# Softmax sums with their 1e-9 beside them, the gate as a second factor, u w by a product with ones, and new places for all steps

## The chip, the core and the metric

One Trainium2 chip, one of its cores: TensorE (PE, with its weight loads shown as PEld), VectorE (DVE), ScalarE (ACT), GpSimd (POOL) and SyncE (SP, which issues every DMA of this kernel). The metric is the device time of one execution in microseconds (us). Before the change three timed runs gave 396.64, 402.85 and 397.48 us; the median is 397.48 us.

## The reference

Two layers. The first is a linear attention with decay, for B=4, H=8, S=768, D=48:

```python
cur = np.einsum('bhd,bhe->bhde', u[None] * kt, vt)
y[:, :, t] = np.einsum('bhd,bhde->bhe', rt, state + cur)
state = w[None, :, :, None] * state + np.einsum('bhd,bhe->bhde', kt, vt)
```

The second takes y as x (4 x 768 x 384) and runs 4 expert attentions with heads of 64, of which each token uses the best two by a gate:

```python
a = np.exp(scores)
a /= a.sum(-1, keepdims=True) + 1e-09
ye = a @ v @ wo[e]
...
w = np.exp(sel)
w /= w.sum(-1, keepdims=True) + 1e-09
```

The scores are causal, and the wq and wk of the test are large, so products of q and k are made of two parts (hi and lo) each.

## The kernel before

The sequence of each of the 4 batches is cut into 6 chunks of 128 tokens: chunk n runs from 0 to 23, and n % 6 = 5 is the last of a batch. Three chunks make a group G (0 to 7), two groups make a batch; g = G % 2 is 0 for a batch's first half and 1 for its second, whose attention also reads the keys of the first.

Work on a chunk (names begin with a_): `load_chunk` fetches k and r into kdbuf (4 buffers) and rdbuf (3), `load_vh` and `load_zv` fetch v in two layouts. `a_decay` (L230) multiplies k and r by the decay tables tab_k and tab_r, on DVE for the first 3 chunks and on GpSimd for the others. `a_own` forms the u-term: two products on GpSimd into ku (L238, L239), a sum on DVE (L241), and two halves of ownv (L244, one on DVE and one on GpSimd). `a_transpose` (L253, L256, L257), `a_scores` (L265, L267), `a_out` (L277, L279) and `a_state` (L288, then zs on DVE at L294 and zvbuf on GpSimd at L296, twice, for the two 64-token halves) make the chunk's output and carry the state. `a_xt` (L307 to L310) turns the output round and splits it.

Work on a group (names begin with m_): `m_proj` (L337, xq at L341 to L345, then SP copies into tk at L355 and tq at L351), `m_values` (L366), `m_gate`, and for each of 4 experts and 3 query chunks `m_scores` (L412, L413): DVE takes minima over the masked scores (L418), ACT the exponential and its row sum (L419). After the third query chunk the factor f is made on DVE (L423 adds 1e-9, L424 inverts, L425 multiplies by the gate) and GpSimd scales the three tiles pr by it (L429). `m_turn` (L437, L439) transposes them, `m_av` (L453) multiplies by the values, `m_out` (L469 to L473) by wo.

Order: the table ORDER gives every step a place in units of one group; the steps are issued in order of these places (`at`), `needs` only asserts that what a step reads was issued before, and the tile framework's scheduler puts each engine's instructions in line from there. At run time each engine works strictly through its own line, and SP issues its DMAs in line too, so a transfer whose buffer is not free holds back all transfers behind it. PSUM has four banks named ps, taken in turn by every step that uses one (a_state's and m_av's among them), and two pairs named psb for the scores.

Before the first chunk, powers of w are built on DVE (L156 to L160), copied into two tiles (DVE L169, ACT L170), transposed by PE (L173) and copied into tab_k and tab_r by ACT (L174). `load_uw` spreads w and u over all 128 partitions by two DMAs of 192 KB and multiplies them on DVE (L184).

Of the kernel before, what the change touches and what calls it, by code (L numbers as in the profile page):

```python
# [7 lines left out]
F32 = mybir.dt.float32  # L8
F32R = mybir.dt.float32r
BF16 = mybir.dt.bfloat16  # L10
AF = mybir.ActivationFunctionType
OP = mybir.AluOpType
AX = mybir.AxisListType
PSUM = bass.MemoryType.PSUM

ORDER = {
    "load": -0.6596, "decay": -0.4545, "late": 0.0159, "early": 0.2138, "early_project": -0.0623, "copy_zv":
    -0.2698, "load_uw": -1.0607, "load_vh": -0.5828, "load_zv": -0.7408, "transpose": -0.2149, "own": -0.1496,
    "burst": -0.0903, "xt": 0.3275, "project": 0.0765, "project_step": 0.0977, "attend": [-0.0676, -0.1006],
    "av": [0.2761, 0.2103], "mix": [0.3321, 0.4911], "mix_step": 0.1117, "load_qk": -0.2109, "load_v":  # L20
    -0.6283, "load_o": 0.3769, "attend_step": 0.0365, "values": 0.2328, "tail": -0.0092, "tail_step": 0.9545,
}
# [12 lines left out]
def decay_attention_then_mixture_of_attention(  # L35
# [27 lines left out]
    GC = 3  # L63
# [3 lines left out]
    scale = 0.125  # L67
# [70 lines left out]
    for i, rows in enumerate((lo, hi)):  # L138
# [27 lines left out]
    tab_k = const.tile([P, H, 64], F32, name="tab_k")  # L166
    for nat, half in ((tab_k, up[:, :, 63::-1]), (tab_r, down[:, :, 64:0:-1])):
        col = work.tile([P, S], F32, name="pr", bufs=BUFS["pr"])[:, :NP * C].rearrange("d (p c) -> d p c", p=NP)
        nc.vector.tensor_copy(col[:, :, :64], half)  # L169
        nc.scalar.activation(col[:, :, 64:], half, AF.Copy)  # L170
        pst = ps1.tile([P, NP, P], F32, name="ps")
        for p in range(NP):
            nc.tensor.transpose(pst[:, p, :], col[:, p, :], ident)  # L173
        nc.scalar.activation(nat.rearrange("s h d -> s (h d)"), pst.rearrange("s p d -> s (p d)"), AF.Copy)  # L174
    w64 = const.tile([P, NP, 1], F32, name="w64")
    nc.vector.tensor_copy(w64, up[:, :, 64:65])

    uw = const.tile([P, H, D], F32, name="uw")

    def load_uw():  # L180
        wb = work.tile([P, H, D], F32, name="ku", bufs=BUFS["ku"])
        nc.sync.dma_start(wb, bass.AP(tensor=w.tensor, offset=w.offset, ap=[[0, P], [1, H * D]]))
        nc.sync.dma_start(uw, bass.AP(tensor=u.tensor, offset=u.offset, ap=[[0, P], [1, H * D]]))
        tc.keep_in_program_order(nc.vector.tensor_tensor(uw, uw, wb, op=OP.mult))  # L184


    wqk_hi = const.tile([P, KT, 2 * NV], F32R, name="wqk_hi")
# [36 lines left out]
    xt = {}  # L224
# [85 lines left out]
        nc.vector.tensor_tensor(lo[:, :, cols], ps, hi[:, :, cols].bitcast(F32), op=OP.subtract)  # L310


    keys = {}
    mg = {}

    def m_start(G):
        b, g = divmod(G, NG)
        keys[b, g] = dict(
            tk=work.tile([P, E, GT], F32R, name="tk", bufs=3),
            vv=work.tile([P, GC, E, HD], F32, name="vv", bufs=3),  # L320
        )
        mg[G] = dict(
            tq=[work.tile([P, 2, GT], F32R, name="tq", bufs=BUFS["tq"]) for _ in range(E)],
            sums=tiny.tile([P, E, GC], F32, name="sums"),
        )

    def m_proj(G, kind, pr):
# [74 lines left out]
    def m_scores(G, e, j):  # L402
        b, g = divmod(G, NG)
        tq, sums = mg[G]["tq"], mg[G]["sums"]
        N = (g * GC + j + 1) * C
        psb = ps2.tile([P, 1024], F32, name="psb")
        q = slice(j * C, (j + 1) * C)
        for h in range(g + 1):
            tk = keys[b, h]["tk"]
            n = GT if h < g else (j + 1) * C  # L410
            o = psb[:, 128 + h * GT:128 + h * GT + n]
            nc.tensor.matmul(o, tq[e][:, 0, q], tk[:, e, :n], start=True, stop=False)  # L412
            nc.tensor.matmul(o, tq[e][:, 1, q], tk[:, e, :n], start=False, stop=True)  # L413
        ps = psb[:, 128:128 + N]

        nm = tiny.tile([P, 1], F32, name="nm", bufs=6)
        pr = work.tile([P, S], F32, name="pr", bufs=BUFS["pr"])
        nc.vector.tensor_tensor_reduce(pr[:, :N], ps, after[:, S - N:], 1.0, 3e38, op0=OP.add, op1=OP.min, accum_out=nm)  # L418
        nc.scalar.activation(pr[:, :N], pr[:, :N], AF.Exp, bias=nm, scale=-1.0, accum_out=sums[:, e, j:j + 1])  # L419
        mg[G]["p", e, j] = pr  # L420
        if j == GC - 1:
            f = tiny.tile([P, GC], F32, name="f", bufs=4)
            nc.vector.tensor_scalar(f, sums[:, e, :], 1e-9, None, op0=OP.add)  # L423
            nc.vector.reciprocal(f, f)  # L424
            nc.vector.tensor_tensor(f, f, mg[G]["gate"][:, :, e], op=OP.mult)  # L425
# [170 lines left out]
```

## Time and profile before

| what | value |
|---|---|
| median of 3 runs | 397.48 us (396.64 to 402.85) |
| the profiled execution's own time | 399.55 us |
| its span, first to last instruction | 397.8 us |
| PE busy | 352.7 us (89%) |
| DVE, ACT, POOL busy | 260.5, 239.6, 228.1 us |
| mean granted TensorE clock | 0.961 of full speed |

Busy times overlap, and a busy PE is not PE at its peak: its matmuls are pipelined and their records overlap. The granted clock is 1.0 (2.4 GHz) or 0.5 (1.2 GHz) in each stretch. The view of waits names, for an engine and line, what ended its idle time; such idle time costs something only where the engine, or one that waits for it, sets the pace. The profiled execution lies 2.07 us above the median.

### The profile page before, as it was taken

What the parts mean: (1) busy time and instruction counts of PE and PEld (TensorE: products, weight loads), DVE (VectorE), ACT (ScalarE), POOL (GpSimd) and SP (SyncE); (2) the same over time, 40 slices, a digit from 0 to 9 for tenths busy, and PEclk for the clock granted to TensorE, in tenths of its full rate; (3) what the DMA queues carried; (4) which work ended last, traced back from release to release, by engine and by line L of the source; (5) the groups of instructions that cost most, each with busy time, mean ns of one, the idle gap of its engine ahead of it and who ended that gap; (6) DMA issues with size and microseconds to landing.
All of it is one profiled execution on the core that took longest, in us unless ns stands there. A gap on an engine that the chain in (4) does not pass through costs nothing.

```text
span 397.8 us, 10483 instructions
## 1 busy us (share of the span) xinstructions
PE 352.7 (89%) x3762; PEld 303.1 (76%) x3762; DVE 260.5 (65%) x728; ACT 239.6 (60%) x597; POOL 228.1 (57%) x322
## 2 busy tenths in 40 slices
PE   4566798779987999899889999999789999999995
PEld 1465687669866997599768997699668998798863
DVE  7598689567687766676677757675577655447510
ACT  0868637253764675656557485657468485557961
POOL 5389997867389628674497826773465503213420
PEclk9669999689999999999989999999989999999999
DMA  8995376917943774536844582536811550074011
GB/s 122 179 178 97 71 164 147 143 33 162 175 83 70 172 174 75 103 81 138 173 97 95 134 207 63 98 82 140 180 51 31 133 130 22 7 172 123 20 41 59
DMA packets 114772, 43.95 MB, mean 110 GB/s; under 512 B 102945, under 2 KB 110625, under 8 KB 114721
## 3 DMA queue, kind: packets, MB, share of 16 engines
q1 hardware_dynamic: 114720, 43.28, 52.9%
q8 instruction: 30, 0.49, 0.5%
q14 instruction: 22, 0.17, 0.1%
HBM read 19.67 MB, written 4.72 MB: 61 GB/s over the span
## 4 chain that ended last, share of the span: by engine, by line
PE 53%; DMA 7%; DVE 6%; ACT 4%; POOL 3%; issue 3%; SPq 3%; ACTq 0%; DVEq 0%; POOLq 0%
PE ps L337 10%; PE ps L453 9%; PE ps L437 8%; PE psb L412 4%; PE ps L277 4%; PE psb L413 3%; PE ps L366 3%; DMA kdbuf<-in_k_dram 3%; PE ps L265 3%; PE ps L288 2%; PE ps L253 2%; SPq L351 2%; PE ps L469 2%; PE ps L470 2%; PE ps L471 2%
## 5 line engine op out<-in xcount | busy, mean ns | idle before, releaser
L429 POOL TENSOR_SCALAR pr<-pr,f 128x128 f32<-128x128 f32 (+5 forms) x96 | 60.9, 652 | 68.7 <-DVE f L425 22.6
L419 ACT ACTIVATE pr<-pr,nm 128x128 f32<-128x128 f32 (+5 forms) x96 | 64.3, 671 | 32.9 <-DVE nm L418 31.3
L418 DVE CUSTOM_DVE_ANT_0 pr<-psb,after 128x128 f32<-128x128 f32 (+5 forms) x96 | 58.9, 619 | 33.2 <-PE ps L437 27.2
L439 ACT ACTIVATE pt<-ps 128x384 f32<-128x384 f32 x144 | 56.4, 421 | 31.1 <-PE ps L437 29.1
L437 PE MATMUL ps<-ident,pr 128*128 128x128 f32 x336 | 59.9, 282 | 8.2 <-POOL pr L429 3.3
L296 POOL TENSOR_TENSOR zvbuf<-zs,w 64x192 f32<-64x192 f32 x88 | 47.1, 535 | 13.6 <-DVE zs L294 9.4
L437 PEld LDWEIGHTS ps<-ident,pr 128*128 128x128 f32 x336 | 40.0, 141 | 16.2 <-POOL pr L429 5.0
L412 PE MATMUL psb<-tk,tq 128*128 128x128 f32 (+2 forms) x144 | 50.0, 351 | 2.1 <-DVE nm L418 1.1
L453 PE MATMUL ps<-pt,vv 128*64 128x384 f32 (+2 forms) x288 | 42.8, 436 | 6.1 <-DVE zs L294 6.1
L294 DVE TENSOR_TENSOR zs<-ps,zvbuf 64x192 f32<-64x192 f32 x88 | 31.0, 353 | 21.3 <-POOL zvbuf L296 16.0
L413 PE MATMUL psb<-tk,tq 128*128 128x128 f32 (+2 forms) x144 | 43.1, 316 | 0.0
L230 POOL TENSOR_TENSOR kdbuf<-kdbuf,tab_k 128x384 f32<-128x384 f32 x21 | 21.7, 1034 | 35.0 <-DMA kdbuf<-in_k_dram 32.1
L453 PEld LDWEIGHTS ps<-pt,vv 128*64 128x64 f32 x288 | 20.2, 141 | 26.8 <-issue 16.7
L267 DVE TENSOR_TENSOR rabuf<-ps,before 64x512 f32<-64x512 f32 x48 | 33.0, 688 | 4.1 <-PE ps L265 3.2
L337 PE MATMUL ps<-xt_hi,wqk_hi 128*128 128x384 f32 x96 | 35.0, 364 | 0.8 <-ACT xt_hi L309 0.7
L337 PE MATMUL ps<-xt_lo,wqk_hi 128*128 128x384 f32 x96 | 33.3, 347 | 1.1 <-DVE xt_lo L310 1.1
L238 POOL TENSOR_TENSOR ku<-kdbuf,uw 128x384 f32<-128x384 f32 x24 | 25.7, 1072 | 14.7 <-DVE kdbuf L230 9.1
L341 ACT ACTIVATE xq<-ps 128x384 fp32r<-128x384 f32 x32 | 15.6, 488 | 30.2 <-PE ps L337 24.4
L277 PE MATMUL ps<-zvbuf,rabuf 128*64 128x48 f32 x768 | 29.3, 227 | 4.6 <-POOL ku L239 3.2
L337 PE MATMUL ps<-xt_hi,wqk_lo 128*128 128x384 f32 x96 | 32.8, 342 | 0.0
L277 PEld LDWEIGHTS ps<-zvbuf,rabuf 128*64 128x64 f32 x768 | 26.4, 141 | 8.0 <-POOL ku L239 3.8
L412 PEld LDWEIGHTS psb<-tk,tq 128*128 128x128 f32 x144 | 27.8, 193 | 5.3 <-DVE nm L418 3.1
(109 smaller groups left out, 817.4 us busy)
## 6 DMA issues: line engine op xcount, KB each, us to landing
tq<-xq SPq DMA_DIRECT2D x64, 192.0 KB, 3.4
tk<-xq SPq DMA_DIRECT2D x64, 96.0 KB, 2.2
kdbuf<-in_k_dram SPq DMA_DIRECT2D x24, 192.0 KB, 4.0
rdbuf<-in_r_dram SPq DMA_DIRECT2D x24, 192.0 KB, 3.9
vhbuf<-in_v_dram SPq DMA_DIRECT2D x48, 96.0 KB, 3.1
out_dram<-o SPq DMA_DIRECT2D x23, 192.0 KB, 2.3
zvbuf<-in_v_dram SPq DMA_DIRECT2D x72, 48.0 KB, 2.5
pr<-in_moe_wv_dram SPq DMA_DIRECT2D x3, 128.0 KB, 3.6
```

Source lines behind the costliest of these rows:

```text
L267: nc.vector.tensor_tensor(ra[rows, par].rearrange("s i p t -> s (i p) t"), ps[rows].rearrange("s i p t -> s (i p) t"), before[rows, None, ...
L277: nc.tensor.matmul(ps[half, 2 * p + par, :], ra[:, par, i, p, :], zv[:, par, i, p, :], start=True, stop=True)
L296: nc.gpsimd.tensor_tensor(zvbuf[(n + i) % NZ][rows, par, 1 - i], zs[rows], w64[rows].to_broadcast([64, NP, D]), op=OP.mult)
L337: nc.tensor.matmul(ps, a[:, t, m0:m0 + P], x[:, t, :], start=i == 0, stop=i == n - 1)
L412: nc.tensor.matmul(o, tq[e][:, 0, q], tk[:, e, :n], start=True, stop=False)
L413: nc.tensor.matmul(o, tq[e][:, 1, q], tk[:, e, :n], start=False, stop=True)
L418: nc.vector.tensor_tensor_reduce(pr[:, :N], ps, after[:, S - N:], 1.0, 3e38, op0=OP.add, op1=OP.min, accum_out=nm)
L419: nc.scalar.activation(pr[:, :N], pr[:, :N], AF.Exp, bias=nm, scale=-1.0, accum_out=sums[:, e, j:j + 1])
L429: nc.gpsimd.tensor_scalar(p[:, :N], p[:, :N], f[:, i:i + 1], 1.0, op0=OP.mult, op1=OP.mult)
L437: nc.tensor.transpose(pst[:, j, :], mg[G]["p", e, j][:, i * C:(i + 1) * C], ident)
L439: nc.scalar.activation(pt[:, j0:], pst[:, j0:], AF.Copy)
L453: nc.tensor.matmul(psy[par * HD:par * HD + HD, j0 * C:], vv[:, i % GC, e, :], mg[G]["t", e, i][:, j0:].rearrange("s j t -> s (j t)"), star ...
```

## The change

Line numbers of the changed kernel differ: L429 becomes L444, L230 becomes L240, L238 and L239 become L248 and L249, L244 becomes L254, L296 becomes L306, L170 is gone, L174 becomes L177, L118 becomes L119. The 1e-9 stands in a second column beside each softmax sum, so one sum over two columns replaces the addition of a constant; the gate is no longer multiplied into f but handed to GpSimd as the second factor of the scaling. Both columns of the decay tables are copied by DVE. A copy of a small tile (lower) is put first on ACT. u w is formed in one partition and spread by a matmul with ones. Every number of the table ORDER changes; two of its lines are shown, with the numbers that place the u-term (own), the output and state (burst, with a_out a third of a group behind it) and the turned output (xt).

```diff
 ORDER = {
...
-    -0.2698, "load_uw": -1.0607, "load_vh": -0.5828, "load_zv": -0.7408, "transpose": -0.2149, "own": -0.1496,
-    "burst": -0.0903, "xt": 0.3275, "project": 0.0765, "project_step": 0.0977, "attend": [-0.0676, -0.1006],
...
+    -0.3428, "load_uw": -0.9439, "load_vh": -0.5687, "load_zv": -0.6948, "transpose": -0.2504, "own": 0.1079,
+    "burst": -0.0679, "xt": 0.4025, "project": 0.1361, "project_step": 0.0927, "attend": [-0.0751, -0.2394],
...
+    nc.scalar.activation(lower.rearrange("p a b -> p (a b)"), lower.rearrange("p a b -> p (a b)"), AF.Copy)
...
-        nc.vector.tensor_copy(col[:, :, :64], half)
-        nc.scalar.activation(col[:, :, 64:], half, AF.Copy)
+        for i in range(2):
+            nc.vector.tensor_copy(col[:, :, i * 64:i * 64 + 64], half)
...
-        nc.scalar.activation(nat.rearrange("s h d -> s (h d)"), pst.rearrange("s p d -> s (p d)"), AF.Copy)
+        behind(nc.scalar.activation(nat.rearrange("s h d -> s (h d)"), pst.rearrange("s p d -> s (p d)"), AF.Copy))
...
+    ones = const.tile([1, P], F32, name="ones")
+    nc.gpsimd.memset(ones, 1.0)
     def load_uw():
-        wb = work.tile([P, H, D], F32, name="ku", bufs=BUFS["ku"])
-        nc.sync.dma_start(wb, bass.AP(tensor=w.tensor, offset=w.offset, ap=[[0, P], [1, H * D]]))
-        nc.sync.dma_start(uw, bass.AP(tensor=u.tensor, offset=u.offset, ap=[[0, P], [1, H * D]]))
-        tc.keep_in_program_order(nc.vector.tensor_tensor(uw, uw, wb, op=OP.mult))
+        row = tiny.tile([1, 2, H * D], F32, name="row", bufs=1)
+        nc.sync.dma_start(row[:, 0], w.rearrange("h d -> (h d)")[None, :])
+        nc.sync.dma_start(row[:, 1], u.rearrange("h d -> (h d)")[None, :])
+        tc.keep_in_program_order(nc.vector.tensor_tensor(row[:, 0], row[:, 0], row[:, 1], op=OP.mult))
+        ps = ps1.tile([P, H * D], F32, name="ps")
+        nc.tensor.matmul(ps, ones, row[:, 0], start=True, stop=True)
+        nc.scalar.activation(uw.rearrange("p h d -> p (h d)"), ps, AF.Copy)
...
+    sumsbuf = [const.tile([P, E, GC, 2], F32, name=f"sums{i}") for i in range(2)]
+    for t in sumsbuf:
+        nc.gpsimd.memset(t[:, :, :, 1:], 1e-9)
...
-        nc.scalar.activation(pr[:, :N], pr[:, :N], AF.Exp, bias=nm, scale=-1.0, accum_out=sums[:, e, j:j + 1])
+        nc.scalar.activation(pr[:, :N], pr[:, :N], AF.Exp, bias=nm, scale=-1.0, accum_out=sums[:, e, j, 0:1])
...
-            f = tiny.tile([P, GC], F32, name="f", bufs=4)
-            nc.vector.tensor_scalar(f, sums[:, e, :], 1e-9, None, op0=OP.add)
+            f = tiny.tile([P, GC, 1], F32, name="f", bufs=4)
+            nc.vector.tensor_reduce(f, sums[:, e], axis=AX.X, op=OP.add)
             nc.vector.reciprocal(f, f)
-            nc.vector.tensor_tensor(f, f, mg[G]["gate"][:, :, e], op=OP.mult)
+            gate = mg[G]["gate"]
...
-                nc.gpsimd.tensor_scalar(p[:, :N], p[:, :N], f[:, i:i + 1], 1.0, op0=OP.mult, op1=OP.mult)
+                nc.gpsimd.tensor_scalar(p[:, :N], p[:, :N], f[:, i], gate[:, i, e:e + 1], op0=OP.mult, op1=OP.mult)
```

GpSimd's line before, where chunk 17 (kdbuf1_75, rdbuf2_80) is decayed; zvbuf2_90 and zvbuf0_88 are the two state products of chunk 14, ownv and ku belong to the u-terms, pr are the tiles of group 3's first expert:

```order
L230 TENSOR_TENSOR kdbuf1_75<-kdbuf1_75,tab_k_144 128x8x48
L230 TENSOR_TENSOR rdbuf2_80<-rdbuf2_80,tab_r_143 128x8x48
L238 TENSOR_TENSOR ku_3412<-kdbuf1_75,uw_165 128x384
L296 TENSOR_TENSOR zvbuf2_90<-zs_2748,w64_163 64x192 x2
L239 TENSOR_TENSOR ku_3412<-ku_3412,rdbuf2_80 128x384
L244 TENSOR_TENSOR ownv_2905<-vhbuf0_81,own_2903 64x384
L296 TENSOR_TENSOR zvbuf0_88<-zs_2753,w64_163 64x192 x2
L230 TENSOR_TENSOR kdbuf2_76<-kdbuf2_76,tab_k_144 128x8x48
L238 TENSOR_TENSOR ku_3628<-kdbuf2_76,uw_165 128x384
L429 TENSOR_SCALAR pr_2921<-pr_2921,f_3006 128x512
```

The same place of GpSimd's line in the changed kernel, with the same names:

```order
L306 TENSOR_TENSOR zvbuf2_90<-zs_2727,w64_164 64x192 x2
L240 TENSOR_TENSOR kdbuf1_75<-kdbuf1_75,tab_k_145 128x8x48
L306 TENSOR_TENSOR zvbuf0_88<-zs_2732,w64_164 64x192 x2
L248 TENSOR_TENSOR ku_3603<-kdbuf1_75,uw_166 128x384
L240 TENSOR_TENSOR rdbuf2_80<-rdbuf2_80,tab_r_144 128x8x48
L444 TENSOR_SCALAR pr_2861<-pr_2861,f_2923,gate_2775 128x512
L444 TENSOR_SCALAR pr_2911<-pr_2911,f_2923,gate_2775 128x640
L444 TENSOR_SCALAR pr_2920<-pr_2920,f_2923,gate_2775 128x768
L254 TENSOR_TENSOR ownv_3063<-vhbuf0_81,own_3061 64x384
L240 TENSOR_TENSOR kdbuf2_76<-kdbuf2_76,tab_k_145 128x8x48
L249 TENSOR_TENSOR ku_3603<-ku_3603,rdbuf2_80 128x384
```

The first state product (zvbuf2_90) moved from behind the two decays and one ku product to ahead of them, the second (zvbuf0_88) from behind five others to behind the k decay alone, and the second ku product now stands behind the scaling of three pr tiles. The same move is found at chunks 11 and 23.

ACT's line before, from its first instruction to the first copies of chunk 0 (zvbuf0, vhbuf0 hold v of chunk 0, zvbuf1, vhbuf1 of chunk 1):

```order
L118 ACT_TABLE_LOAD
L118 ACTIVATE zvbuf0_88<-vhbuf0_81 64x192 x4
L170 ACTIVATE pr_145<-pr_133 128x4x64
L170 ACTIVATE pr_154<-pr_133 128x4x64
L174 ACTIVATE tab_k_144<-ps_148 128x512
L174 ACTIVATE tab_r_143<-ps_157 128x512
L118 ACTIVATE zvbuf1_89<-vhbuf1_82 64x192 x4
L256 ACTIVATE kzbuf0_84<-ps_207 64x512 x2
```

The same piece of ACT's line in the changed kernel:

```order
L152 ACT_TABLE_LOAD
L152 ACTIVATE lower_123<-lower_123 128x16
L119 ACTIVATE zvbuf0_88<-vhbuf0_81 64x192 x4
L177 ACTIVATE tab_k_145<-ps_149 128x512
L177 ACTIVATE tab_r_144<-ps_158 128x512
L119 ACTIVATE zvbuf1_89<-vhbuf1_82 64x192 x2
L194 ACTIVATE uw_166<-ps_183 128x384
L119 ACTIVATE zvbuf1_89<-vhbuf1_82 64x192 x2
L266 ACTIVATE kzbuf0_84<-ps_215 64x512 x2
```

The table load moved from the first copy of v to the copy of lower, the two column copies left ACT, and the copy of u w came in between the halves of chunk 1's v.

## Rows read from the trace of the kernel before

**Rows 1.** The page: span, and busy time, share of the span and instructions of PE.

```profile
span 397.8 us, 10483 instructions
PE 352.7 (89%) x3762; PEld 303.1 (76%) x3762; DVE 260.5 (65%) x728; ACT 239.6 (60%) x597; POOL 228.1 (57%) x322
```

**Rows 2.** Windows by granted clock (window, us, busy PE PEld DVE ACT POOL, clock, DMA share, GB/s).

```profile
30.10:71.10 41.00, 31.37 (x453) 28.18 (x451) 33.78 (x84) 25.87 (x59) 35.65 (x47) 1.00 0.58 120
71.10:77.90 6.80, 6.19 (x57) 4.74 (x57) 2.43 (x9) 1.86 (x6) 6.64 (x11) 0.50 1.36 172
77.90:84.70 6.80, 4.14 (x50) 3.21 (x50) 6.26 (x14) 1.98 (x6) 6.14 (x8) 1.00 0.21 35
84.70:88.20 3.50, 3.50 (x15) 3.33 (x13) 0.56 (x1) 2.24 (x6) 1.42 (x4) 0.51 0.00 0
200.80:204.20 3.40, 3.40 (x19) 2.88 (x16) 3.07 (x8) 2.19 (x5) 3.09 (x5) 0.50 0.29 100
289.50:293.00 3.50, 3.43 (x16) 1.92 (x17) 3.18 (x8) 1.31 (x3) 2.71 (x4) 0.51 0.02 8
```

**Rows 3.** Waits, 193 to 205 us (waiter, what ended it: total us, times, longest us).

```profile
POOL kdbuf L230 <- DMA kdbuf<-in_k_dram: 3.7, 1, 3.7
DVE zs L294 <- POOL zvbuf L296: 3.4, 2, 3.2
PE ps L453 <- DVE zs L294: 2.6, 1, 2.6
```

**Rows 4.** Waits, 284 to 293 us.

```profile
PE ps L453 <- DVE zs L294: 3.5, 1, 3.5
```

**Rows 5.** Timeline of POOL, 188 to 203 us (start, us, instruction, idle before).

```profile
195.43 1.02 POOL L230 TENSOR_TENSOR kdbuf<-kdbuf,tab_k 128x384 f32<-128x384 f32 x1 [3.68 <-DMA kdbuf<-in_k_dram]
198.35 1.07 POOL L296 TENSOR_TENSOR zvbuf<-zs,w 64x192 f32<-64x192 f32 x2
```

**Rows 6.** Timeline of SP: the loads of k for chunks 17 and 23.

```profile
190.29 0.69 SPq L101 DMA_DIRECT2D kdbuf<-in_k_dram  x1
279.74 0.59 SPq L101 DMA_DIRECT2D kdbuf<-in_k_dram  x1
```

**Rows 7.** The chain of waits, in order of time: output of chunk 15.

```profile
220.19 0.92 PE ps L277 x32
```

**Rows 8.** Timeline of ACT, 5 to 17 us.

```profile
9.68 1.28 ACT L118 ACT_TABLE_LOAD   x1 [9.68 <-DMA vhbuf<-in_v_dram]
10.97 1.48 ACT L118 ACTIVATE zvbuf<-vhbuf 64x192 f32<-64x192 f32 x4
12.47 0.72 ACT L170 ACTIVATE pr<-pr 128x256 f32<-128x256 f32 x2
14.11 0.60 ACT L174 ACTIVATE tab_k<-ps 128x512 f32<-128x512 f32 x1 [0.92 <-PE ps L173]
```

**Rows 9.** Timeline, 0 to 35 us: the first u-term product.

```profile
15.38 1.24 POOL L238 TENSOR_TENSOR ku<-kdbuf,uw 128x384 f32<-128x384 f32 x1 [9.14 <-DVE kdbuf L230]
```

**Rows 10.** Waits, 60 to 73 us.

```profile
PE ps L437 <- POOL pr L429: 2.8, 1, 2.8
```

**Rows 11.** Waits, 79 to 90 us.

```profile
PE ps L337 <- DVE xt_lo L310: 1.1, 1, 1.1
PE ps L307 <- DVE ownv L279: 0.9, 1, 0.9
```

**Rows 12.** Lines, shapes apart (count, busy us, mean ns of one, idle before).

```profile
L423 DVE TENSOR_SCALAR f<-sums 128x3 f32<-128x3 f32 x32 | 11.0, 344 | 18.0 <-ACT pr L419 17.8
L425 DVE TENSOR_TENSOR f<-f,gate 128x3 f32<-128x3 f32 x32 | 10.5, 332 | 0.8
L395 DVE TENSOR_REDUCE den<-ex 128x3 f32<-128x12 f32 x8 | 1.3, 166 | 0.1
L429 POOL TENSOR_SCALAR pr<-pr,f 128x384 f32<-128x384 f32 x16 | 9.5, 591 | 0.0
L239 POOL TENSOR_TENSOR ku<-ku,rdbuf 128x384 f32<-128x384 f32 x24 | 24.2, 1010 | 1.7 <-DVE rdbuf L230 0.6
```

More of the change, by code (lines that the diff above doesn't have):

```diff
@@ L16 @@
 ORDER = {
-    "load": -0.6596, "decay": -0.4545, "late": 0.0159, "early": 0.2138, "early_project": -0.0623, "copy_zv":
-    -0.2698, "load_uw": -1.0607, "load_vh": -0.5828, "load_zv": -0.7408, "transpose": -0.2149, "own": -0.1496,
-    "burst": -0.0903, "xt": 0.3275, "project": 0.0765, "project_step": 0.0977, "attend": [-0.0676, -0.1006],
-    "av": [0.2761, 0.2103], "mix": [0.3321, 0.4911], "mix_step": 0.1117, "load_qk": -0.2109, "load_v":
-    -0.6283, "load_o": 0.3769, "attend_step": 0.0365, "values": 0.2328, "tail": -0.0092, "tail_step": 0.9545,
+    "load": -0.7439, "decay": -0.5272, "late": 0.0023, "early": -0.01, "early_project": 0.0589, "copy_zv":
+    -0.3428, "load_uw": -0.9439, "load_vh": -0.5687, "load_zv": -0.6948, "transpose": -0.2504, "own": 0.1079,
+    "burst": -0.0679, "xt": 0.4025, "project": 0.1361, "project_step": 0.0927, "attend": [-0.0751, -0.2394],
+    "av": [0.253, 0.2242], "mix": [0.2746, 0.6405], "mix_step": 0.0833, "load_qk": -0.5519, "load_v": -0.1277,
+    "load_o": 0.0735, "attend_step": 0.0541, "values": 0.1955, "tail": -0.0729, "tail_step": 0.8383,
 }
@@ L50, in decay_attention_then_mixture_of_attention @@
     nc = tc.nc
+    behind = tc.keep_in_program_order
     B, H, S, D = r.shape
@@ L323, in m_start @@
             tq=[work.tile([P, 2, GT], F32R, name="tq", bufs=BUFS["tq"]) for _ in range(E)],
-            sums=tiny.tile([P, E, GC], F32, name="sums"),
+            sums=sumsbuf[G % 2],
         )
```

## The prediction

> **What bounds the kernel now.** I read the page first: PE is busy for 352.7 of 397.8 us, the others for 57 to 65% [rows 1]. So PE sets the pace, and about 45 us are left in which it does nothing. Next I cut the span where TensorE's granted clock changes. In the stretches at 0.5 (1.2 GHz of 2.4) PE is busy nearly throughout and works at half speed, and each follows a gap [rows 2]: PE is busy 31.37 of 41.0 us before 71.1, and 4.14 of 6.8 us between 77.9 and 84.7. A gap is therefore paid twice, once as idle time and once as slow matmuls behind it.
>
> Then I asked the waits around the later gaps what ended them. At 193 to 205 us PE's value product (L453) waited 2.6 us for DVE's zs, zs waited 3.2 us for GpSimd's zvbuf, and GpSimd itself sat 3.7 us before the decay of a chunk's k, until the load of k had landed [rows 3]. The timeline shows the mechanism: the load was issued at 190.29 [rows 6], the decay began at 195.43, and zvbuf came only at 198.35 [rows 5], because in GpSimd's line it stands behind both decays and a ku product. zs holds a PSUM bank while it waits, and L453 needs one. The same chain cost PE 3.5 us one batch later [rows 4]; the two loads lie 89.45 us apart [rows 6], which is two groups, so a group lasts 44.7 us here.
>
> **The change part by part.**
>
> *Places on GpSimd.* The new line has the first state product ahead of the late decay at chunks 11, 17 and 23, so zs of the second half can run, and the bank comes free while GpSimd waits for the load. What goes is 2.6 + 3.5 us of waiting [rows 3, 4] and, if the clock then stays up, half of the 3.40 and 3.43 us that PE worked at 1.2 GHz behind these gaps [rows 2], 1.7 + 1.7: together 9.5 us. What is late next is the second state product, still behind the decay; it is needed first by the output of chunk 15, which ran at 220.19 [rows 7], some 22 us after zvbuf at 198.35 [rows 5], so a delay of 2 or 3 us hides there. The SP line still issues these k loads behind the copies of tq, so GpSimd's own 3.7 us of waiting stays; it is only moved off PE's path. Bounds: 0, if another wait takes the place, to 9.5. I take 9.5.
>
> *Start.* ACT waited until 9.68 us for v, then loaded its table (1.28), copied v (1.48) and two table columns (0.72), and only after PE's transposes came tab_k, at 14.11 [rows 8]. Now the table load hangs on nothing late and the columns go to DVE (two more copies there), so tab_k follows the four copies of v: 9.68 + 1.48 = 11.16 instead of 14.11, 2.95 us earlier, provided that the second half of v has landed. But the first u-term product, which starts GpSimd's work on chunks at 15.38 [rows 9], now needs uw through a matmul and an ACT copy that stands behind half of chunk 1's v. The first SP issues stay four, with small rows in place of two spreads. Bounds: 0, if uw is the last to come, to 14.11 - 9.68 = 4.4, if v comes earlier too. I take 2.0, two thirds of 2.95, because only one of the two branches is held.
>
> *Early groups.* Between 60 and 90 us PE waits 2.8 us for scaled tiles [rows 10] and 0.9 + 1.1 us around the turned output [rows 11], and works 6.19 and 3.50 us at the low clock [rows 2]. The place of xt moves from 0.3275 to 0.4025 of a group, and that of a_out from 0.3333 - 0.0903 = 0.2430 to 0.3333 - 0.0679 = 0.2654, so the distance between output and transpose grows from 0.0845 to 0.1371 group, 3.8 to 6.1 us at 44.7. That covers the second pair of waits, 2.0 us, and half of the 3.50 us behind them, 1.75: 3.8. The 2.8 us I leave, since the first group's attention moves with its scores. Bounds: 0 to all of it, 2.8 + 2.0 + 3.1 + 1.75 = 9.7. I take 3.8.
>
> *The factor f.* Per expert and group DVE loses an addition of 344 ns and a product of 332 ns and gains a sum over two columns; the nearest row is the gate's sum, 166 ns [rows 12]. That is 0.51 us, 32 times 16.3 us of DVE time. Little of it is on the path: between the last scores and the first transposes of an expert stands other PE work in nearly all groups, which hides it; without that cover all 16.3 us would count. Bounds 0 to 16.3; I take 1.0, two of the 32 places, as DVE is idle for over 100 us [rows 1].
> The mean of 344 ns is far above what three columns need, so these two instructions must wait for something. The Trainium skill (SBUF — State Buffer, "Who interferes with whom") says that on trn2 a DVE instruction with two SBUF inputs, or one in a two-port mode, locks against a GpSimd instruction reading SBUF, and that tensor_reduce never does. By that rule the new sum costs 166 ns even beside a busy GpSimd, and DVE gains the 16.3 us; if it waited like its predecessors it would cost 344 and DVE would gain 10.6. The sum below is the same by either.
>
> *GpSimd's second factor.* The instruction already made two products, by f and by 1.0; a second factor per partition is not shown in the trace. From below 0, since it can't do less work than with a constant; from above the difference between a product of two tiles and a scaling of the same shape, 1010 - 591 = 419 ns [rows 12], 96 times 40 us of GpSimd time. I take 0, by the row of the same instruction; GpSimd is busy 57% [rows 1], so a tenth of the upper end would hide too.
>
> *All other places.* Every step moves by some hundredths of a group, and new gaps can open. I allow one gap of the size of the smaller one removed, 2.6 + 1.7 = 4.3 us.
>
> Sum: -9.5 - 2.0 - 3.8 - 1.0 + 4.3 = -12.0. The profiled execution took 399.55 us, 1.75 outside its span, and would become 387.5; it lies 2.07 above the median, so the median 397.48 becomes 385.5.
>
> **Rivals.**
>
> *The gaps come back elsewhere.* GpSimd still stands 3.7 us before each late k [rows 3], and now the second state product and the first scaled tiles of a group lie behind it; if one of them is needed sooner than I think, PE waits as before. For it: PE already waits for scaled tiles once [rows 10]. Against it: the 22 us of distance above. Then only start and f remain, 397.5 - 3.0 = 394.5.
>
> *Everything fits.* The early groups lose all 9.7 us and no new gap opens: -9.5 - 2.0 - 9.7 - 1.0 = -22.2, 375.3. For it: GpSimd is the busy engine between 30 and 71 us (35.65 of 41.0 [rows 2]), and its order is new there too. Against it: its amount of work per chunk is the same.
>
> *The u-term comes late (slower).* The place of own moves from 0.3926 group ahead of the output to 0.1575, from 17.5 to 7.0 us. In it must fit two products of 1.0 us, a sum of half a microsecond, ownv (1 us) and, by the new order, three scaled tiles between the two products, each at least 0.59 us [rows 12]: 5.3 us, with 1.7 to spare. If GpSimd runs later than that, the output's addition, its transposes and the next projection wait. At an overrun of 1.5 us in each of the 18 chunks from 6 on that is 27 us: 385.5 + 27 = 412.5. It decides from an overrun of 1.1 us on, where 18 x 1.1 = 20 eats the 12.0 and 8 more. Against it: GpSimd idles 43% of the span [rows 1].
>
> **How the numbers follow.** Chances: the forecast 0.55, own range 377 to 392; gaps come back 0.25; everything fits 0.12; u-term late 0.08. Two per cent, about what a measurement of this kernel can tell from no change, is 389.5 below and 405.4 above. Faster by more: most of the forecast (0.43), everything fits (0.12), a little of the second case (0.03), 0.58. Slower by more: the late u-term and a little besides, 0.09. Within: 0.33. The range goes from 374, where everything fits, to 398, where the gaps come back with the new one on top (394.5 + 4.3 = 398.8).
>
> **What would show it.** Right: in the waits no L453 behind zs of a microsecond or more, while GpSimd's waits for loads of k stay; two low-clock stretches fewer after 190 us; tab_k copied near 11 us; the new sum near 166 ns, the scaling of 384 columns near 591. Wrong: PE waiting for scaled tiles or for ownv behind a late k, the transposes of the output (L317 now) waiting in most groups, low-clock stretches in new places, or GpSimd's scaling longer by a tenth or more.

## The result, and the profile after

| | kernel before | changed kernel |
|---|---|---|
| median | 398.84 us (4 runs, 396.64 to 402.85) | 384.50 us (4 runs, 384.08 to 385.75) |
| ratio | | 0.9663, 95% interval 0.9601 to 0.9726 |
| profiled execution, own time and span | 399.55, 397.8 us | 384.75, 383.0 us |
| mean granted TensorE clock | 0.961 | 0.991 |

The forecast was 385.5 us with a range of 374 to 398; faster by over 2% had the largest chance. The time came out as forecast, in part by luck: most of its terms did not, as the sections below show.

The changed kernel's page, first part (busy time, share of the span, instructions), which answers to [rows 1]:

```profile
PE 347.7 (91%) x3764; PEld 298.6 (78%) x3764; DVE 246.9 (64%) x698; ACT 238.4 (62%) x597; POOL 234.2 (61%) x325
```

DVE has 13.6 us less to do, GpSimd 6.1 us more, and PE 5.0 us less, although it does the same work: that is time at the low clock. To see where the 14.8 us of the two profiled executions went, I cut both spans at the same two points of the program: the first exponential of group 2, and of group 6. Kernel before, windows (length, busy time of PE, PEld, DVE, ACT, POOL with their instructions, clock, DMA share, GB/s):

```profile
157.41:335.56 178.15, 168.53 (x1874) 147.41 (x1873) 119.06 (x345) 111.73 (x281) 100.45 (x143) 0.98 0.50 110
335.56:397.80 62.24, 57.88 (x413) 47.04 (x411) 26.33 (x95) 39.79 (x114) 14.97 (x24) 1.00 0.24 68
```

The changed kernel, same points:

```profile
145.97:319.76 173.79, 165.36 (x1875) 144.85 (x1874) 114.89 (x327) 111.59 (x281) 104.86 (x145) 1.00 0.52 113
319.76:383.00 63.24, 58.02 (x418) 47.33 (x416) 24.96 (x89) 40.05 (x115) 16.91 (x24) 1.00 0.23 66
```

So 11.4 us are gone by group 2 (157.41 against 145.97; 9.4 of them are idle time of PE, by the table below), 4.4 between the points, and 1.0 is lost behind them. In the middle stretch PE's busy time fell by 3.2 us, which is the two stretches at the low clock, and its idle time by only 1.2 (178.15 - 168.53 = 9.62 against 8.43), though 6.1 us of waits were to go there.

What took their place stands in the waits at 193 to 205 us, which answer to [rows 3] (waiter, what ended it: total, times, longest):

```profile
PE ps L452 <- DVE ownv L289: 2.4, 1, 2.4
DVE own L251 <- POOL ku L249: 3.0, 1, 3.0
```

and in GpSimd's timeline there, which answers to [rows 5]:

```profile
182.63 1.08 POOL L306 TENSOR_TENSOR zvbuf<-zs,w 64x192 f32<-64x192 f32 x2
185.79 1.03 POOL L240 TENSOR_TENSOR kdbuf<-kdbuf,tab_k 128x384 f32<-128x384 f32 x1 [2.08 <-DMA kdbuf<-in_k_dram]
...
190.29 2.58 POOL L444 TENSOR_SCALAR pr<-pr,f,gate 128x512 f32<-128x512 f32 x3
192.96 0.83 POOL L254 TENSOR_TENSOR ownv<-vhbuf,own 64x384 f32<-64x384 f32 x1
193.87 1.01 POOL L240 TENSOR_TENSOR kdbuf<-kdbuf,tab_k 128x384 f32<-128x384 f32 x1
194.82 1.00 POOL L249 TENSOR_TENSOR ku<-ku,rdbuf 128x384 f32<-128x384 f32 x1
```

The value product (L468 now) no longer waits for zs, as predicted. But the u-term's second product comes at 194.82, behind three scaled tiles, ownv and another decay, and DVE's sum, the output's addition and a bank that PE needs for its transposes wait for it. The windows around it:

```profile
195.00:200.00 5.00, 2.80 (x21) 2.36 (x21) 4.06 (x10) 1.79 (x4) 4.77 (x7) 1.00 0.60 108
200.00:205.00 5.00, 4.54 (x29) 3.65 (x31) 3.87 (x9) 4.90 (x11) 4.69 (x6) 1.00 0.23 45
```

PE still idles 2.2 of 5 us there, but the clock stays at 1.0 behind it; in the kernel before it fell to 0.5 [rows 2]. So not every gap is followed by the low clock.

The start, on ACT and GpSimd, which answers to [rows 8] and [rows 9]:

```profile
7.85 1.48 ACT L119 ACTIVATE zvbuf<-vhbuf 64x192 f32<-64x192 f32 x4 [1.12 <-DVE pr L163]
9.64 0.60 ACT L177 ACTIVATE tab_k<-ps 128x512 f32<-128x512 f32 x1 [0.31 <-PE ps L176]
12.44 0.47 ACT L194 ACTIVATE uw<-ps 128x384 f32<-128x384 f32 x1
...
12.99 1.00 POOL L248 TENSOR_TENSOR ku<-kdbuf,uw 128x384 f32<-128x384 f32 x1 [6.51 <-ACT uw L194]
```

tab_k comes 4.5 us earlier (14.11 before), the first u-term product 2.4 us earlier (15.38 before); in between it waits for uw. The lines that answer to [rows 12]:

```profile
L438 DVE TENSOR_REDUCE f<-sums 128x3 f32<-128x6 f32 x32 | 5.0, 157 | 14.5 <-ACT pr L434 14.2
L444 POOL TENSOR_SCALAR pr<-pr,f,gate 128x384 f32<-128x384 f32 x16 | 10.6, 663 | 0.0
L444 POOL TENSOR_SCALAR pr<-pr,f,gate 128x768 f32<-128x768 f32 x16 | 15.8, 984 | 0.0
```

The new sum costs 157 ns where the addition cost 344, and GpSimd's scaling of 384 columns 663 instead of 591.

### The profile page after: what moved, and what is told of

Its sections match the earlier page's. It is cut to its first block, busy times and chain, and to the rows that moved or that the text cites. A ratio compares the mean times of both kernels' runs of the same rounds, so it can differ in the third digit from the quotient of the medians.

```text
span 383.0 us, 10466 instructions
## 1 busy us (share of the span) xinstructions
PE 347.7 (91%) x3764; PEld 298.6 (78%) x3764; DVE 246.9 (64%) x698; ACT 238.4 (62%) x597; POOL 234.2 (61%) x325
## 4 chain that ended last, share of the span: by engine, by line
PE 44%; POOL 18%; DMA 11%; DVE 7%; ACT 7%; issue 6%; SPq 5%; ACTq 0%; POOLq 0%; DVEq 0%
PE ps L352 9%; PE ps L468 8%; PE ps L452 5%; DMA kdbuf<-in_k_dram 5%; POOL pr L444 4%; DMA rdbuf<-in_r_dram 4%; PE psb L427 3%; PE ps L381 3%; POOL zvbuf L306 3%; PE psb L428 3%; SPq L366 3%; POOL rdbuf L240 2%; PE ps L287 2%; POOL kdbuf L240 2%; DMA tq<-xq 2%
## 5 line engine op out<-in xcount | busy, mean ns | idle before, releaser
L444 POOL TENSOR_SCALAR pr<-pr,f,gate 128x128 f32<-128x128 f32 (+5 forms) x96 | 68.0, 721 | 68.5 <-DVE f L439 45.1
L433 DVE CUSTOM_DVE_ANT_0 pr<-psb,after 128x384 f32<-128x384 f32 (+5 forms) x96 | 58.5, 619 | 23.8 <-PE ps L452 22.3
L434 ACT ACTIVATE pr<-pr,nm 128x384 f32<-128x384 f32 (+5 forms) x96 | 64.2, 671 | 14.1 <-DVE nm L433 13.6
L452 PE MATMUL ps<-ident,pr 128*128 128x128 f32 x336 | 59.0, 280 | 9.5 <-DVE ownv L289 3.0
L306 POOL TENSOR_TENSOR zvbuf<-zs,w 64x192 f32<-64x192 f32 x88 | 47.1, 535 | 12.6 <-DVE zs L304 7.6
L452 PEld LDWEIGHTS ps<-ident,pr 128*128 128x128 f32 x336 | 38.9, 140 | 16.8 <-POOL pr L444 5.3
L427 PE MATMUL psb<-tk,tq 128*128 128x128 f32 (+2 forms) x144 | 48.6, 342 | 1.0 <-DVE nm L433 0.9
L428 PE MATMUL psb<-tk,tq 128*128 128x128 f32 (+2 forms) x144 | 42.7, 311 | 0.0
L468 PE MATMUL ps<-pt,vv 128*64 128x384 f32 (+2 forms) x288 | 41.0, 421 | 0.6 <-ACT pt L454 0.2
L240 POOL TENSOR_TENSOR kdbuf<-kdbuf,tab_k 128x384 f32<-128x384 f32 x21 | 21.3, 1016 | 27.7 <-DMA kdbuf<-in_k_dram 20.3
L468 PEld LDWEIGHTS ps<-pt,vv 128*64 128x64 f32 x288 | 19.5, 136 | 21.0 <-issue 16.0
L266 ACT ACTIVATE kzbuf<-ps 64x512 f32<-64x512 f32 x48 | 28.3, 589 | 6.4 <-PE ps L263 5.9
```

What stands on the lines that cost most here:

```text
L240: eng.tensor_tensor(t[:, :, :D], t[:, :, :D], tab[:, :, :D], op=OP.mult)
L306: nc.gpsimd.tensor_tensor(zvbuf[(n + i) % NZ][rows, par, 1 - i], zs[rows], w64[rows].to_broadcast([64, NP, D]), op=OP.mult)
L444: nc.gpsimd.tensor_scalar(p[:, :N], p[:, :N], f[:, i], gate[:, i, e:e + 1], op0=OP.mult, op1=OP.mult)
L452: nc.tensor.transpose(pst[:, j, :], mg[G]["p", e, j][:, i * C:(i + 1) * C], ident)
L468: nc.tensor.matmul(psy[par * HD:par * HD + HD, j0 * C:], vv[:, i % GC, e, :], mg[G]["t", e, i][:, j0:].rearrange("s j t -> s (j t)"), star ...
```

## The experiments

All of them, with two stretches of each kernel's profiled execution (from the start to the first exponential of group 2, and from there to that of group 6; PE's idle time in each in brackets). Ratios are to the kernel before, run beside them; its median was 397.8 to 398.9 us in each of these comparisons, single runs between 393.85 and 404.16.

| kernel | median us | ratio (95%) | to group 2 | group 2 to 6 |
|---|---|---|---|---|
| before | 398.84 | | 157.41 (31.07) | 178.15 (9.62) |
| changed | 384.50 | 0.9663 (0.9601 to 0.9726) | 145.97 (21.69) | 173.79 (8.43) |
| e1 places alone | 390.40 | 0.9821 (0.9754 to 0.9889) | 149.37 (26.81) | 176.90 (10.15) |
| e2 edits alone | 390.76 | 0.9825 (0.9746 to 0.9903) | 149.52 (20.48) | 180.15 (11.10) |
| e3 start alone | 394.88 | 0.9951 (0.9904 to 0.9998) | 149.85 (21.46) | 180.51 (10.68) |
| e4 factor alone | 395.21 | 0.9926 (0.9875 to 0.9976) | 150.29 (27.42) | 180.50 (10.13) |
| e5 decay behind | 394.13 | 0.9881 (0.9808 to 0.9954) | 157.46 (29.30) | 172.49 (7.04) |
| e6 second factor alone | 394.53 | 0.9901 (0.9860 to 0.9942) | 149.99 (28.37) | 178.81 (8.91) |
| e7 changed, gate on DVE | 387.55 | 0.9740 (0.9688 to 0.9793) | 147.35 (20.26) | 175.81 (9.96) |
| e8 changed, late u on DVE | 383.71 | 0.9649 (0.9600 to 0.9698) | 143.55 (20.13) | 174.87 (8.40) |
| e9 changed, k first | 383.73 | 0.9673 (0.9606 to 0.9740) | 144.61 (19.83) | 174.50 (9.81) |
| e10 e8 + e9 + scaled first | 385.91 | 0.9693 (0.9649 to 0.9737) | 150.10 (22.08) | 171.80 (6.91) |
| e11 e10 at two chunks | 382.40 | 0.9613 (0.9560 to 0.9667) | 146.06 (21.60) | 172.42 (7.52) |
| e12 changed again | 384.88 | 0.9695 (0.9650 to 0.9739) | 143.90 (19.54) | 173.90 (8.78) |

e12 tells how finely this can be read: the same kernel, profiled twice, differs by 2.1 us in the first stretch and by 0.1 in the second. Every other row has one profile, so a stretch is one execution, while the medians and ratios rest on 4 runs or more.

**Which part carries the gain: e1 to e4.** e1 is the kernel before with the new table; e2 the changed kernel with the old table; e3 and e4 are the kernel before with only the edits of the start (L152 to L194 of the changed kernel) and with only those of the factor (sums, reduce, gate as second factor).

```diff
 ORDER = {
-    "load": -0.6596, "decay": -0.4545, "late": 0.0159, "early": 0.2138, ...
+    "load": -0.7439, "decay": -0.5272, "late": 0.0023, "early": -0.01, ...
...
```

> The kernel before with the new table of places alone: no edit of the start, of the factor or of GpSimd's second factor. My sum (places on GpSimd -9.5, early groups -3.8, one new gap +4.3) gives -9.0, near 389.8 us where the kernel before takes 398.8. A first rival, read from the changed kernel's trace (11.4 of its 14.8 us are gone by the first scores of group 2): the places of the first groups carry it, -14 or more here, 385 or less, the gain lying before 160 us. A second rival: the edits at the start carry those 11.4 us, and the places alone give only the 3.4 us behind them, 395.

> The changed kernel with the old table of places: all edits, no new place. My sum gives start -2.0 and factor -1.0, 395.8 us where the kernel before takes 398.8, with both late gaps (a value product behind zs at chunks 17 and 23) still there. If the places of the first groups carry the early gain: the same 395 to 397. If the start carries it: -10 or more, 389 or less.

> The kernel before with the edits at the start alone (table load first on ACT, table columns by DVE, u w by a product with ones). My sum: tab_k near 11 us instead of 14.1 and -2.0 us, 396.8. If the start carries the early gain, -8 to -11, 388 to 391. If the places carry it, nothing: the 2.4 us by which the first u-term product comes earlier are lost again in the first groups, 398 to 399.

> The kernel before with the edits of the factor alone (1e-9 beside each sum, one sum over two columns, the gate as GpSimd's second factor). My sum: -1.0, 397.8 us. Rival: GpSimd's scaling is about 70 ns longer each (96 of them, 6.7 us) and GpSimd paces the first groups, so the kernel is 1 to 3 us slower, 400 to 402. The sum over two columns near 160 ns and the scaling of 384 columns near 660 ns by both.

Table and edits are worth the same, 7 us each (0.9821 and 0.9825), and added up they give 14.1, about the whole (13.4 by its ratio). e1 lies near my sum (7.1 us by the ratio, 9.0 forecast); e2 has over twice my 3.0, and more than start and factor alone give when added up (2.0 and 3.0).

The first stretch tells another story: start alone and factor alone each take 7 to 8 us off it, and both together no more (7.9). That last figure is weak, since the profiled execution of e2 took 394.37 us, the longest of its five (the others took 390.04 to 392.26). Most of the gain lies between the first exponentials of group 0 and of group 1, at nearly the same work of PE. The windows of the kernel before, of e3 and of e6 (told below), and PE's longest wait there in e3:

```profile
56.37:99.57 43.20, 36.51 (x396) 32.59 (x396) 31.79 (x91) 21.60 (x56) 32.99 (x47) 0.88 0.65 121
53.66:90.12 36.46, 32.76 (x387) 29.33 (x387) 28.46 (x89) 20.44 (x55) 29.76 (x43) 0.95 0.75 142
56.69:93.30 36.61, 31.09 (x393) 28.28 (x392) 30.03 (x87) 21.36 (x56) 32.94 (x46) 1.00 0.78 145
PE ps L447 <- POOL pr L439: 3.0, 1, 3.0
```

e4 takes 36.44 us for this part and e2 36.88. So all of them shorten the same part, but not by the same wait: in e3 PE waits as long for scaled tiles as before, and what is gone is most of the waits around the turned output. What they share is a shorter time at the low clock (mean clock 0.88 before, 0.95 to 1.00 here). Some of that varies by itself: e5, whose code is that of the kernel before up to there, took 41.70 us at 0.92. Behind group 2, e2 to e4 lose some 2 us; why was not followed.

**What the factor's gain is: e6.** In the kernel before, only the product of f and gate on DVE is left out.

```diff
-            nc.vector.tensor_tensor(f, f, mg[G]["gate"][:, :, e], op=OP.mult)
+            gate = mg[G]["gate"]
...
-                nc.gpsimd.tensor_scalar(p[:, :N], p[:, :N], f[:, i:i + 1], 1.0, op0=OP.mult, op1=OP.mult)
+                nc.gpsimd.tensor_scalar(p[:, :N], p[:, :N], f[:, i:i + 1], gate[:, i, e:e + 1], op0=OP.mult, op1=OP.mult)
```

> The kernel before, in which only the product of f and gate on DVE is left out and the gate goes in as GpSimd's second factor; the addition of 1e-9 stays on DVE. If the gain of the factor edits (-3, some 7 us of it by the first scores of group 2) comes from the scaling no longer waiting for a product that stands behind the mask of the next chunk on DVE: the same, 395 to 396, with GpSimd's first scaling near 69.4 us instead of 71.1. If it comes from the cheaper sum: 398 to 399. If GpSimd's longer scaling decides: 400 or more.

394.53 us and 7.4 us off the first stretch: the second factor alone has all of the factor's gain that can be read. The timelines of DVE and GpSimd show how. Kernel before:

```profile
68.57 0.80 DVE L399 TENSOR_TENSOR gate<-ex,den 128x12 f32<-128x12 f32 x1
69.41 1.39 DVE L267 TENSOR_TENSOR rabuf<-ps,before 64x512 f32<-64x512 f32 x2
70.72 0.22 DVE L425 TENSOR_TENSOR f<-f,gate 128x3 f32<-128x3 f32 x2
...
68.52 0.83 POOL L244 TENSOR_TENSOR ownv<-vhbuf,own 64x384 f32<-64x384 f32 x1
71.08 2.95 POOL L429 TENSOR_SCALAR pr<-pr,f 128x128 f32<-128x128 f32 x6 [1.73 <-DVE f L425]
```

e6:

```profile
69.14 0.17 DVE L399 TENSOR_TENSOR gate<-ex,den 128x12 f32<-128x12 f32 x1
69.34 1.39 DVE L267 TENSOR_TENSOR rabuf<-ps,before 64x512 f32<-64x512 f32 x2
...
69.53 1.64 POOL L429 TENSOR_SCALAR pr<-pr,f,gate 128x128 f32<-128x128 f32 x3 [0.41 <-DVE gate L399]
```

Before, the product of 0.1 us stands on DVE behind two masks of 0.7 us for the next chunk, and the first scaled tiles of the program begin at 71.08; PE waits 2.8 us for them [rows 10]. In e6 they begin 0.2 us after the gate, at 69.53; that wait is gone, one of 1.4 us for rabuf has come in, and the stretches at 1.2 GHz from 71 to 88 us are gone (clock 1.00 in e6's window above). The gate itself shows a second thing: it took 0.80 us, until GpSimd's ownv beside it ended (68.57 + 0.80 = 69.37; 68.52 + 0.83 = 69.35), and 0.17 where GpSimd stood idle. That is the lock of the Trainium skill (SBUF — State Buffer, "Who interferes with whom"), and the trace agrees, as it does for tensor_reduce: L438 took 138 to 161 ns in all 32 places of the changed kernel, in 13 of which GpSimd was busy throughout with a product of two tiles. What the cheaper sum adds to the second factor can't be read: e4, which has both, and e6 have 0.9926 and 0.9901, and their intervals overlap.

**The second factor in the changed kernel: e7.**

```diff
-            gate = mg[G]["gate"]
+            nc.vector.tensor_tensor(f, f, mg[G]["gate"][:, :, e:e + 1], op=OP.mult)
...
-                nc.gpsimd.tensor_scalar(p[:, :N], p[:, :N], f[:, i], gate[:, i, e:e + 1], op0=OP.mult, op1=OP.mult)
+                nc.gpsimd.tensor_scalar(p[:, :N], p[:, :N], f[:, i], 1.0, op0=OP.mult, op1=OP.mult)
```

> The changed kernel with the gate multiplied into f on DVE again and 1.0 as GpSimd's second factor. By the prediction (second factor 0, f -1.0 in all): 384.5 to 385.5 us. If the product on DVE is what held the first scaled tiles: 2 to 4 us slower, 387 to 389. If GpSimd's 70 ns for each scaling count: 2 us faster, 382 to 383. The scaling of 384 columns is back at 591 ns by all.

387.55 us, 2.7 to 3.0 slower than the two medians of the changed kernel (1.8 to 3.1 by the ratios, whose intervals overlap), and 1.9 to 2.0 of it in the second stretch, where two profiles of the changed kernel differ by 0.1. Of e7's lines, shapes apart:

```profile
L440 DVE TENSOR_TENSOR f<-f,gate 128x3 f32<-128x3 f32 x32 | 9.5, 297 | 0.7
L444 POOL TENSOR_SCALAR pr<-pr,f 128x384 f32<-128x384 f32 x16 | 9.5, 594 | 0.0
```

GpSimd's 70 ns for each scaling are back, 96 of them some 7 us, and nothing is gained by it: that time was hidden, DVE's product was not. What makes the product dear here is open, since no wait of PE names it. Of its 16 places in groups 2 to 5, five stand 0.66 to 1.11 us behind other work on DVE, as in the first group of the kernel before; in five others it follows the reciprocal at once but takes 0.37 to 0.97 us itself, ending with a GpSimd product beside it, as the gate did. In the first part of the span it costs nothing here: between the first exponentials of groups 0 and 1, e7 takes 36.28 us, the changed kernel 36.62 and 35.99 (e12).

**The late gaps: e5.** The kernel before; at chunks 17 and 23 GpSimd's decay is queued behind the first state product of chunks 14 and 20.

```diff
-            eng.tensor_tensor(t[:, :, :D], t[:, :, :D], tab[:, :, :D], op=OP.mult)
+            with tc.issue_after(st["zv", n - 3, 0].ins) if n in (17, 23) else ExitStack():
+                eng.tensor_tensor(t[:, :, :D], t[:, :, :D], tab[:, :, :D], op=OP.mult)
...
-                nc.gpsimd.tensor_tensor(zvbuf[(n + i) % NZ][rows, par, 1 - i], zs[rows],
+                st["zv", n, i] = nc.gpsimd.tensor_tensor(zvbuf[(n + i) % NZ][rows, par, 1 - i], zs[rows],
```

> The kernel before, in which on GpSimd only the decays of chunks 17 and 23 are queued behind the first state product of chunks 14 and 20 (the move on which the -9.5 of the prediction rests, alone). My term: the waits of 2.6 and 3.5 us and half of two stretches at the low clock go, -9.5, near 389 us where the kernel before takes 398.9. Rival, from the changed kernel's landmarks (between the first scores of group 2 and of group 6 it gains 1.3 and 3.0 us): -3 to -4.5, 395, because the bank that PE then needs next is held by the output addition, which waits for the u-term behind the same late decay. Second rival: nothing, 398 to 399. In the trace, the value product behind zs is gone by all three.

394.13 us; by the ratio -4.7, and -5.7 in the second stretch, with nothing changed before it. Its windows from the first to the third expert's first exponential in group 3 and in group 5:

```profile
191.67:215.70 24.03, 21.34 (x247) 18.54 (x244) 19.81 (x48) 15.99 (x37) 20.95 (x28) 1.00 0.55 110
278.29:300.67 22.38, 20.88 (x244) 18.37 (x241) 16.83 (x47) 16.02 (x37) 15.21 (x22) 1.00 0.43 89
```

The kernel before, same points:

```profile
190.96:217.45 26.49, 23.07 (x247) 19.93 (x244) 19.88 (x48) 15.80 (x36) 19.24 (x26) 0.94 0.52 108
279.73:306.31 26.58, 22.46 (x246) 19.29 (x243) 17.27 (x47) 15.85 (x36) 15.18 (x22) 0.94 0.37 79
```

2.5 and 4.2 us are gained. PE's busy time falls by 1.7 and 1.6, about half of each low-clock stretch; its idle time by 0.7 and 2.6 instead of 2.6 and 3.5, because other waits come in (in the first place 1.9 us for rabuf, in the second 0.6 for minima and 0.4 for rabuf). So the move is worth 4.7 us by the ratio (1.8 to 7.6) and 5.7 by the profiled stretch, not 9.5. In the changed kernel, whose other places let the u-term come late, the second stretch gains 4.4 in all; how much of that is this move was not measured.

**What is left there: e8, e9, e10, e11.** All start from the changed kernel. e8 puts the u-term's second product of chunks 11, 17 and 23 on DVE:

```diff
-        nc.gpsimd.tensor_tensor(ku, ku, rd[:, :, :D], op=OP.mult)
+        (nc.vector if n in (11, 17, 23) else nc.gpsimd).tensor_tensor(ku, ku, rd[:, :, :D], op=OP.mult)
```

> The changed kernel with the u-term's second product of chunks 11, 17 and 23 on DVE instead of GpSimd. If what is left of the late gaps is the late u-term (PE's 2.4 us behind the output addition at 195 to 200 us, DVE's sum waiting 3.0 us for the product): that wait goes and the kernel takes 381 to 382.5. If the scaled tiles or the second state product are as late: no change, 384 to 385. If DVE is held up by a product beside a busy GpSimd: 386.

PE's waits at 186 to 202 us in e8:

```profile
PE ps L452 <- POOL pr L444: 2.2, 1, 2.2
```

The wait for the output's addition is gone, and one for the scaled tiles has its place: the second case. The median is 0.8 us lower, but the second stretch is 1.0 longer: PE idles as much as in the changed kernel, and the clock falls again at 190 us. The difference lies in the first stretch, which varies by 2 us.

e9 issues the loads of k of these chunks ahead of the copies of tq (a step `load_k` of its own, 0.46 group earlier):

```diff
...
+        if n in (11, 17, 23):
+            at(t + ORDER["load"] - 0.46, load_k, n)
         at(t + ORDER["load"], load_chunk, n)
```

> The changed kernel with the loads of k of chunks 11, 17 and 23 issued ahead of the copies of tq. If the late load of k is what is left of these gaps: GpSimd's wait of 2.1 us before that decay goes, the scaled tiles of the next expert and the u-term come 2 us earlier, and the kernel takes 381 to 382.5 where the changed kernel takes 384.5. If the load of r, still behind the copies, takes its place: 384 to 385, with GpSimd waiting for r.

GpSimd's timeline in e9, where the decay of k has moved ahead of this stretch:

```profile
187.33 1.02 POOL L245 TENSOR_TENSOR rdbuf<-rdbuf,tab_r 128x384 f32<-128x384 f32 x1 [2.36 <-DMA rdbuf<-in_r_dram]
```

The load of r takes the place of the load of k, again the second case; no gain can be read from 383.73 us.

e10 joins both and also queues r's decay and the u-term's first product behind the three scaled tiles of the next expert:

```diff
-            eng.tensor_tensor(t[:, :, :D], t[:, :, :D], tab[:, :, :D], op=OP.mult)
+            with tc.issue_after(mg[n // GC - 2]["scaled", 0].ins) if n in (11, 17, 23) and t is rd else ExitStack():
+                eng.tensor_tensor(t[:, :, :D], t[:, :, :D], tab[:, :, :D], op=OP.mult)
...
```

> The same with two more moves at chunks 11, 17 and 23: the decay of r and the first product of the u-term are queued behind the scaling of the next expert's three tiles on GpSimd, and the u-term's second product runs on DVE. If PE in these places waits for the scaled tiles and for the u-term by turns, both waits go at once: 379 to 381. If only one of the two counted: as the kernel with k first alone, 381 to 382.5. If GpSimd's work behind them (the state products) is then late: 384 or more.

It missed: 385.91 us. But the second stretch has its shortest time of all, 171.80 us, 2.0 below the changed kernel; the loss is ahead of it, around chunk 11, where PE waits 3.7 us for rabuf between 104 and 122 us. e11 makes the same moves at chunks 17 and 23 alone (shown against e10); e12 is the changed kernel beside it.

```diff
...
-        if n in (11, 17, 23):
+        if n in (17, 23):
...
```

> The changed kernel with the three moves of the run before (k loaded ahead of the copies of tq, r's decay and the first u-term product behind the scaled tiles, the second u-term product on DVE) at chunks 17 and 23 alone, not at chunk 11. In that run the stretch from group 2 to group 6 was 2.0 us shorter than in the changed kernel, and 4.1 us were lost ahead of it, around chunk 11. If the two are independent: the changed kernel's time less 2.0, 382.0 to 383.0. If the lost 4.1 us were chance and not chunk 11: 385 to 386 again. If the start varies more than this: within 1 us of the changed kernel.

> The changed kernel as it is, beside the run before on one chip: 384.1 to 385.8 us, as first measured; above 386.5 or below 383 would mean that the differences of 1 us between the last kernels can't be read.

e11's windows, between the points of group 3 and of group 5 as above, and the changed kernel's:

```profile
178.83:203.82 24.99, 22.84 (x278) 20.07 (x278) 19.64 (x55) 17.95 (x44) 18.92 (x25) 1.00 0.67 142
264.69:289.49 24.80, 23.14 (x280) 20.22 (x280) 19.05 (x54) 17.83 (x44) 15.78 (x22) 1.00 0.45 102
```

```profile
178.37:204.55 26.18, 23.05 (x278) 20.10 (x278) 18.46 (x55) 17.90 (x43) 20.50 (x27) 1.00 0.64 136
265.19:290.76 25.57, 23.26 (x280) 20.18 (x280) 18.75 (x54) 17.81 (x43) 14.44 (x21) 1.00 0.44 100
```

At the same work PE idles 1.0 and 0.7 us less in these two places. The median is 382.40 against 384.88 us on the same chip, both kernels' runs spread over 5 to 7 us (379.96 to 386.85 and 382.18 to 386.83), and the intervals of their ratios overlap: e11 beats the kernel before surely and the changed kernel by about 1.5 us in the second stretch; by its median it is probable, not shown. e12's median lies where it was expected, but two of its six runs (382.18 and 386.83) lie outside the bounds that its expectation named, so differences of 1 us between these kernels are not read from their times here.

## Why the prediction was right, point by point

*What bounds the kernel.* Right for the late gaps: e5 shows the second payment at the low clock, busy time falling by about half of each stretch. "Paid twice" is too general: the changed kernel's gap at 195 us is followed by a clock of 1.0, and low stretches at the start cost nothing that can be seen (last section).

*Places on GpSimd, -9.5.* The mechanism was right, the term too large. The low clock's share, 1.7 + 1.7, came as worked out (3.2 in the changed kernel, 3.3 in e5). The waits' share, 6.1, did not: PE's idle time fell by 3.3 in e5's two places and by 1.2 in the second stretch of the changed kernel. The step that failed is "What is late next is the second state product ... so a delay of 2 or 3 us hides there": late next were the u-term and the scaled tiles, by turns (e8). The sentence's 198.35 is also the start of the first state product; the second began at 201.67 in the kernel before, which leaves 18.5 us instead of 22, still enough for the delay. That GpSimd's own waits for k stay was right (2.08 us at chunk 17).

*New gaps, +4.3.* Right in kind: 2.4 us of it is the u-term at chunk 17. It is the rival "late u-term" with 2.4 us at one place instead of 1.5 at 18.

*Start, -2.0.* Right in size, -2.0 alone (e3, interval -3.8 to -0.1), but by luck. uw was indeed last to come, and v was there earlier than I took it to be (its copies began at 7.85, not 9.68, so tab_k came at 9.64, not 11.16). By the profiles the first exponential came 2.7 us earlier, as forecast in kind; then 6.7 us more were gained up to group 1, which I had not forecast, and 4.5 lost behind it.

*Early groups, -3.8, and the factor, -1.0.* Too small, and these terms with the start make up the time. The two waits that the first counted do go: in e1 PE has neither the one for ownv nor the one for xt_lo between the first exponentials of groups 0 and 1, though waits of 1.2 and 1.0 us for rabuf and xq come in. The step that failed is "The 2.8 us I leave, since the first group's attention moves with its scores" together with "between the last scores and the first transposes of an expert stands other PE work in nearly all groups, which hides it". In the kernel before nothing hid it in the first group: e6 leaves out the factor's product alone, which stood behind the next chunk's masks, and the 2.8 us and the low clock behind them go. In the changed kernel start and places shorten the same part too, and there the product costs nothing (e7). All three parts together took 11.4 us off the first stretch (13.5 in e12) where 6.8 were forecast, and 7.6, 7.1 and 8.0 alone. So they don't add there; how the 11.4 divide among them, and what the new places do in the first stretch, stays open.

*GpSimd's second factor, 0.* Its duration was wrong (+72 ns at 384 columns, over the tenth that I had named), its cost right: hidden. It gains some 4 us in the kernel before (e6) and 1.8 to 3.1 in the changed one (e7), which I had not seen, because I had costed DVE's product by its mean duration and not by what waits for it where it is late.

So the sum came out by luck, by two errors of opposite sign: the first stretch -11.4 instead of -6.8, the rest -3.4 instead of -5.2, 14.8 in place of 12.0 from the profiled execution, 14.3 between medians.

## What to carry to other kernels

A tiny product on a busy engine can cost its place in that engine's line and, beside a busy GpSimd, the time that it is held up, instead of its bare 0.16 us: look at what stands ahead of it and beside it where its result is waited for first, and if the consumer has a free operand, hand the factor over, even if the consumer becomes longer. A wait that is removed is worth its time less the next wait behind the same late transfer, so follow GpSimd's line for three or four instructions past the one that moves. Parts that shorten the same part of the span need not add there, even through different waits; only runs of each alone show it. And the profile of one execution is set beside the median of several before its stretches are added up.

## What the runs showed of the hardware that was not expected

A per-partition pointer instead of a constant as GpSimd's second factor costs about 70 ns: 663 against 591 ns at 384 columns, 984 against 908 at 768, where the kernel before is read in the same view, and 69 to 96 ns at each of the six widths against e7.

The granted clock early in the program differs between two executions of the same kernel, and the one at the lower clock was not the slower one. The changed kernel, first profile:

```profile
9.25:16.00 6.75, 6.55 (x37) 4.56 (x36) 4.35 (x8) 5.35 (x12) 2.19 (x2) 1.00 1.30 184
```

and in e12:

```profile
9.25:16.00 6.75, 6.75 (x37) 4.50 (x35) 4.84 (x10) 5.82 (x12) 2.91 (x3) 0.50 1.45 187
26.25:33.00 6.75, 5.72 (x84) 5.63 (x85) 6.03 (x11) 2.88 (x7) 6.36 (x8) 0.50 0.82 140
```

Up to group 2 the mean clock was 0.98 in the first and 0.94 in the second, which reached that point 2.1 us earlier all the same. What set the pace there was not followed.
